# New planner limits for a mixed-attention kernel whose instruction order is made by a list scheduler

## Chip, cores and metric

The kernel runs on one core of one Trainium2 chip. The metric is device time in microseconds of one execution, as the median of several runs. A lower time is better.

## The reference

The input is one sequence of 2048 positions with 512 features. Two attention branches with 32 heads of 16 features each read it, and a gate per position mixes their outputs:

```python
def reference(A_x, A_wqkv, A_wo, B_x, B_wqkv, B_wo, gate_w):
    def _A_ref(x, wqkv, wo):
...
        scores = jnp.einsum("bhqd,bhkd->bhqk", q, k) * scale
        p = _softmax(scores, axis=-1)
        o = jnp.einsum("bhqk,bhkd->bhqd", p, v)
...
    def _B_ref(x, wqkv, wo):
...
        W, dil = 8, 2
...
        idx = pos[:, None] - off[None, :]
...
        logits = jnp.einsum("bhsd,bhswd->bhsw", q, kg) * scale
        logits = jnp.where(mask[None, None, :, :], logits, -1e9)
        attn = _softmax(logits, axis=-1)
        o = jnp.einsum("bhsw,bhswd->bhsd", attn, vg)
...
    x = A_x
    g = _sigmoid((x * gate_w).sum(-1, keepdims=True))
    a = _A_ref(x, A_wqkv, A_wo)
    b = _B_ref(x, B_wqkv, B_wo)
    return g * a + (1 - g) * b
```

Branch A is full attention: 32 heads times 2048x2048 scores, each of which needs an exponential. Branch B looks at 8 positions per query, two apart, so it is small next to A.

## The kernel before

**Items.** Branch A's scores are cut into 2048 *items*. An item is one head, 512 queries and 128 keys: a score matmul writes 128x512 f32 values into one PSUM bank (L1801), an engine takes the exponential into SBUF, and a value matmul multiplies the result with V and adds it to an accumulator bank (L1605). Thirty-two blocks of 64 items follow each other; a block is four heads by 512 queries by 16 key tiles. The four score matmuls of a group lie in four row strips of TensorE (PE), the four value matmuls in four column strips, so four run beside each other.

**Two ways to an exponential.** ScalarE (ACT) computes exps exactly, in one instruction for two or three items side by side (L1855); its two PSUM slots are three and two banks wide, and the planner may lend the third bank of the wide slot out, which makes that exp two items wide. VectorE (DVE) can take an item too: a first pass turns the scores into 16-bit integers that, read as f16, approximate the exponential (L1533), and for every batch of up to four items two later passes make shifted copies (L1539, in a tile called yb). The three pieces are summed by three value matmuls with weighted copies of V, so a DVE item has three value matmuls where an ACT item has one. Only 6 of the 16 key tiles (KD) may go to DVE, and none in the last items of a block.

**The rest.** Projections for Q, K and V of both branches run on PE (L881) and are evacuated by DVE, out of a pool of four banks called flex that DVE items and block accumulators use too. After a block DVE normalises it (L1628 on). Branch B multiplies Q with shifted K, sums, takes a softmax, writes weights and V to DRAM, reads them back in shifted form, and GpSimd (POOL) multiplies them (L1332); PE sums these products (L1350) and DVE evacuates them (L1355). Output tiles are projected on PE near the end, B's half first. When little PE work has been issued lately, the planner inserts matmuls on zeros to keep TensorE's activity up (L1517). A second, exact version of the kernel stands behind a flag and doesn't run with these inputs.

**What sets the order.** The order of all engines' instructions is made on the host, while the program is being built, by `run` (L1460 on). It is a list scheduler: it keeps a model time for each engine (`t`), takes the engine that is furthest behind, and lets it issue the best candidate. `p` counts items whose score matmul has been issued. Other work is a list of steps, each with an engine, a cost, predecessors, an item number before which it may not start (`rel`), one by which it is wanted (`due`), and a class for DVE. The chip's engines then run their queues in that order and wait for each other through semaphores; a wrong cost in the model can't break the result, but it can leave an engine waiting.

**The limits.** Eleven limits steer the choices. Each has five levels (`LEVELS`, L55), and a digit per stretch of 32 items picks the level (`STRETCH`, L68; 64 stretches). `tune(k)` (L1498) gives the level in force. What they do:

- `backlog`, `backlog_s`, `misc_slack` (L1724 to L1736, `d_wanted`): a DVE item is taken only while the DVE work that is queued or ready within 1.5 us costs less than `backlog` us, and while no step that needs a bank is due by `p + misc_slack`. `backlog_s` takes the place of `backlog` where only the lending of a bank is decided.
- `lend` (L1907): when the wide slot's third bank is lent: 1, if a DVE item is wanted; 2, if a step that needs a bank is due; 3, either; 4 and more, always.
- `grab` (L1913): how many DVE items may ride with one score burst. `alone` (L1978): the margin in time for a DVE item's score matmul by itself.
- `part_us` (L1948): after how many us a value group of fewer than four goes. `urgent` (L1946): other PE steps go ahead of value matmuls once due within so many items. `fit` (L1934): PE starts other work only if that ends no more than `fit` us after the next ACT slot is expected to come free.
- `port` (L1891): how much other DVE work must be at hand before POOL may start a product, because POOL and DVE's fast passes are kept apart in time by explicit dependencies.
- `order` (L1876): the rank of DVE's step classes: first transpose of a finished block, evacuations, first passes on items, later passes, background.

The two lines in which an item is taken or refused:

```python
            load = max(0.0, t["DVE"] - now) + sum(s.cost for s in ready if s.eng == "DVE")
            return load < tune("backlog" if flex else "backlog_s")
```

Of the kernel before, what the change touches and what calls it, by code (L numbers as in the profile page):

```python
# [55 lines left out]
    backlog=(1.5, 2.2, 3.0, 3.8, 5.0),  # L56
    backlog_s=(0.5, 1.0, 1.5, 2.2, 3.0),
    part_us=(1.5, 2.2, 3.0, 4.0, 6.0),
    misc_slack=(-20, -8, 0, 8, 20),
    urgent=(0, 4, 8, 16, 32),  # L60
    fit=(-0.2, 0.0, 0.2, 0.4, 0.6),
    port=(0.3, 0.6, 0.9, 1.2, 2.0),
    alone=(-9.0, -0.2, 0.0, 0.2, 9.0),
    grab=(0, 1, 4, 2, 1),
    lend=(0, 1, 3, 2, 7),
    order=((-1, 1, 0, 2, 3), (-1, 0, 2, 1, 3), (-1, 0, 1, 2, 3), (-1, 0, 1, 2, 1), (1, 0, 1, 2, 3)),
)
STRETCH = dict(  # L68
    backlog="4213224322422022220413433124322022122202222223242202222212220022",
    backlog_s="2202222312432222422021322322222202212222042122213222222022222323",  # L70
    part_us="2220421041243222243202020241242042211223124202210222222222222220",
    misc_slack="0004233313424222221242320140240224120321112121323222222242210222",
    urgent="2322222222200222222212213221431222034112012232322222222021222222",
    fit="2421222322244222322212212022422212421422222223222222222022222222",
    port="2223222202243220222020324222224422222202222222221322222222341322",
    alone="2211222122222114022222243221222222221322242231222232222233302222",
    grab="1222212222214222222222222222222224411342244213222222222422422422",
    lend="4220222222233202222224132222224232322212222244232122222242311422",
    order="2222432212022222320131412123232222203202222120223222222222222222",
)  # L80
SLOT_D = 3
D_LAST = 58
# [1957 lines left out]
```

## Time and profile before

| what | value |
|---|---|
| time, median of 4 runs | 736.44 us (735.89 to 736.94) |
| the profiled execution: its time | 736.56 us |
| the profiled execution: span from first to last instruction | 734.8 us |
| mean granted TensorE clock | 0.997 |
| DVE items (first passes, L1533) | 501 |
| exps on ACT, two items wide / three wide | 484 / 193 |
| ACT's exps, busy | 707.8 us |
| POOL's products of branch B (L1332) | 128, from 414.8 to 700.3 us |
| DMA | 48.53 MB, mean 66 GB/s |

The page gives busy time per engine as the union of its instructions' spans. ACT's and DVE's instructions overlap a little at their ends, so the mean of one instruction times their number is more than the busy time of the group; the distance between two starts is shorter than an instruction's span. PE's spans are modelled at their ends, and a busy PE is not PE at its peak. A group's line has the source line, engine, operation, tiles, shapes and count, then busy us, the mean ns of one, the engine's idle time just before them, and what ended it.

### The profile page before, as it was taken

What the parts mean: (1) busy time and instruction counts of PE and PEld (TensorE: products, weight loads), DVE (VectorE), ACT (ScalarE), POOL (GpSimd) and SP (SyncE); (2) the same over time, 40 slices, a digit from 0 to 9 for tenths busy, and PEclk for the clock granted to TensorE, in tenths of its full rate; (3) what the DMA queues carried; (4) which work ended last, traced back from release to release, by engine and by line L of the source; (5) the groups of instructions that cost most, each with busy time, mean ns of one, the idle gap of its engine ahead of it and who ended that gap; (6) DMA issues with size and microseconds to landing.
All of it is one profiled execution on the core that took longest, in us unless ns stands there. A gap on an engine that the chain in (4) does not pass through costs nothing.

```text
span 734.8 us, 20496 instructions
## 1 busy us (share of the span) xinstructions
PE 691.0 (94%) x8285; PEld 229.1 (31%) x8285; DVE 653.7 (89%) x1114; ACT 713.3 (97%) x691; POOL 204.6 (28%) x218
## 2 busy tenths in 40 slices
PE   8999999999999999999989998999999999999996
PEld 5333322333332232323222322232223323322333
DVE  6988889986799999998998998999889998899974
ACT  4999999999999999999999999999999999999994
POOL 3143000000002232123000336655543546361500
PEclk9999999999999999999999999999999999999998
DMA  6002000000100100001021455476444465374101
GB/s 166 3 18 70 10 17 9 1 2 2 39 2 14 26 1 3 6 1 38 2 74 72 115 110 153 113 169 163 116 122 125 122 156 130 81 173 121 37 24 35
DMA packets 63718, 48.53 MB, mean 66 GB/s; under 512 B 21760, under 2 KB 63232, under 8 KB 63488
## 3 DMA queue, kind: packets, MB, share of 16 engines
q1 hardware_dynamic: 62912, 45.70, 24.7%
q8 instruction: 67, 1.10, 0.7%
q0 software_dynamic: 288, 1.05, 0.5%
q10 hardware_dynamic: 416, 0.39, 0.2%
q14 instruction: 35, 0.29, 0.2%
HBM read 39.85 MB, written 5.26 MB: 61 GB/s over the span
## 4 chain that ended last, share of the span: by engine, by line
ACT 46%; PE 26%; issue 15%; DVE 9%; DMA 2%; SPq 1%; POOL 0%; ACTq 0%; POOLq 0%
ACT pt L1855 45%; PE fps L1801 10%; PE fps L1605 7%; PE fps L881 7%; DVE yb L1533 4%; DVE yb L1539 2%; DMA vw<-v_dram 1%; SPq L1300 1%; PE fps L1215 1%; SPq L948 1%; ACT er L1220 1%; PE fps L954 0%; PE fps L1350 0%; DVE t L1628 0%; DVE oT L1641 0%
## 5 line engine op out<-in xcount | busy, mean ns | idle before, releaser
L1855 ACT ACTIVATE pt<-fps 128x1024 bf16<-128x1024 f32 (+1 forms) x677 | 707.8, 1244 | 6.6 <-PE fps L1801 5.7
L1533 DVE TENSOR_SCALAR yb<-fps 128x512 int16<-128x512 f32 x501 | 325.6, 682 | 31.7 <-PE fps L1801 30.3
L1801 PE MATMUL fps<-qm,kT 32*128 32x512 bf16 x2048 | 309.9, 382 | 32.8 <-ACT pt L1855 24.4
L1605 PE MATMUL fps<-pt,vaug 128*32 128x512 bf16 (+1 forms) x1646 | 237.3, 373 | 0.7 <-DVE bq L1177 0.5
L1801 PEld LDWEIGHTS <-kT 32*128 32x128 bf16 x2048 | 95.0, 91 | 296.7 <-issue 289.8
L1539 DVE TENSOR_SCALAR yb<-yb 128x2048 int16<-128x2048 int16 (+3 forms) x270 | 169.0, 656 | 0.8
L1605 PE MATMUL fps<-yb,vaugw 128*32 128x512 f16 (+1 forms) x1060 | 160.2, 372 | 0.6 <-DVE yb L1539 0.5
L1332 POOL TENSOR_TENSOR er<-er,vw 128x512 bf16<-128x512 bf16 x64 | 72.7, 1154 | 136.0 <-DMA erb<-er_dram 69.2
L881 PE MATMUL fps<-xT,ww 128*32 128x512 bf16 (+2 forms) x1296 | 97.5, 381 | 0.2
L1605 PEld LDWEIGHTS <-vaug 128*32 128x32 bf16 x2176 | 66.7, 94 | 86.9 <-issue 75.3
L1605 PE MATMUL fps<-yb,vaug 128*32 128x512 f16 (+1 forms) x530 | 92.5, 372 | 0.0
L1332 POOL TENSOR_TENSOR erb<-erb,vw 128x512 bf16<-128x512 bf16 x64 | 72.4, 1155 | 60.7 <-DVE yb L1539 32.8
L1201 POOL TENSOR_TENSOR prod<-bq,bk 128x512 bf16<-128x512 bf16 x32 | 33.8, 1074 | 95.2 <-DVE yb L1539 65.8
L1605 PEld LDWEIGHTS <-vaugw 128*32 128x32 bf16 x1060 | 43.7, 95 | 35.7 <-issue 28.0
L1124 POOL DMA_DIRECT2D wAv<-in_A_wo_dram x1 | 0.8, 754 | 121.7 <-PE fps L881 121.7
L881 PEld LDWEIGHTS <-ww 128*32 128x32 bf16 x1296 | 23.8, 95 | 34.1 <-issue 28.8
L1201 DVE TENSOR_TENSOR prod<-bq,bk 128x2048 bf16<-128x2048 bf16 x24 | 29.3, 1241 | 0.2
L1628 DVE STREAM_TRANSPOSE t<-fps 128x512 f32<-128x512 f32 x32 | 22.7, 709 | 4.2 <-PE fps L1605 4.1
L1517 PE MATMUL fps<-wz 128*32 128x512 bf16 x157 | 21.5, 382 | 0.0
L909 DVE CAST vaug<-fps 128x384 bf16<-128x384 f32 (+1 forms) x24 | 12.2, 510 | 10.2 <-PE fps L881 10.1
L881 PE MATMUL fps<-woB,oB 128*32 128x512 bf16 x256 | 19.6, 383 | 0.3 <-DVE yb L1533 0.2
L881 PE MATMUL fps<-wAv,oT 128*32 128x512 bf16 x256 | 19.6, 384 | 0.1
(112 smaller groups left out, 281.1 us busy)
## 6 DMA issues: line engine op xcount, KB each, us to landing
vw<-v_dram SPq DMA_DIRECT2D x128, 128.0 KB, 3.2
er<-er_dram SPq DMA_DIRECT2D x128, 64.0 KB, 3.0
erb<-er_dram SPq DMA_DIRECT2D x128, 64.0 KB, 3.0
v_dram<-vs SPq DMA_DIRECT2D x16, 128.0 KB, 2.8
out_dram<-ob SPq DMA_DIRECT2D x15, 128.0 KB, 2.6
qm<-qs SPq DMA_DIRECT2D x112, 16.0 KB, 1.8
x_in<-in_A_x_dram SPq DMA_DIRECT2D x3, 512.0 KB, 6.6
ww<-in_B_wqkv_dram SPq DMA_DIRECT2D x12, 128.0 KB, 2.5
```

What stands on the lines that cost most here:

```text
L881: self.nc.tensor.matmul(out=out_ps[32 * c:32 * c + 32, 0:n], lhsT=lhsT_of(c), rhs=rhs, start=start, stop=stop, tile_position=(0, 32 * c))
L909: self.nc.vector.tensor_copy(out=self.vaug4[:, st0:st0 + nst, h0:h1, 0:DH], in_=self.misc[:, 0:nst * n].rearrange("p (t h e) -> p t h e", ...
L948: self.nc.sync.dma_start(out=self.qm[i % NQM][r][k:k + 16, :], in_=self.qs[i % 2][k:k + 16, :])
L1201: return e.tensor_tensor(out=pr[m % 2][:, a:b], in0=bq[ct][:, a:b], in1=bk[ct][:, o + a:o + b], op=ALU.mult)
L1332: return nc.gpsimd.tensor_tensor(out=st_["erb"][m % 4][:, g, :], in0=st_["erb"][m % 4][:, g, :], in1=st_["vw"][m % 2][:, g, :], op=ALU.mult)
L1517: nc.tensor.matmul(out=self.flex[acc[cur]][32 * j:32 * j + 32, :], lhsT=self.wz[:, 0:32], rhs=self.wz[:], start=False, stop=False, tile_po ...
L1533: return nc.vector.tensor_scalar(out=self.yb[bt["buf"]][:, 0, i * 512:(i + 1) * 512], in0=bank[:], scalar1=A, scalar2=1024.0 * (15.0 + PW_ ...
L1539: return nc.vector.tensor_scalar(out=y[:, k, 0:n], in0=y[:, 0, 0:n], scalar1=float(round(1024.0 * (PW_S[k] - PW_S[0]))), scalar2=None, op0 ...
L1605: nc.tensor.matmul(out=out, lhsT=v, rhs=r, start=start, stop=stop, tile_position=(0, 32 * j))
L1628: nc.vector.transpose(out=self.t1[:, par].rearrange("p a b -> p (a b)"), in_=self.flex[acc[b]])
L1801: nc.tensor.matmul(out=dst, lhsT=self.kT[ct % 2][32 * j:32 * j + 32, kt * 128:(kt + 1) * 128], rhs=self.qm[(4 * ct + qc) % NQM][par][32 * ...
L1855: nc.scalar.activation(out=self.pt[pi[0]][pi[1]][:, 0:n * 512], in_=self.aslot[si][:, 0:n, :].rearrange("p a b -> p (a b)"), func=ACT.Exp, ...
```

## The change

Only the digits of `STRETCH` change; `LEVELS`, the step list, the costs in the planner and the code stay. Before, every limit sits at level 2 in most stretches, and 240 of the 704 digits differ from that. After, every limit has one most common level, and 21 digits differ from it. In all, 527 of the 704 digits are others than before.

| limit | most common level before | after |
|---|---|---|
| backlog | 3.0 us | 2.2 us |
| backlog_s | 1.5 us | 2.2 us |
| part_us | 3.0 us | 1.5 us |
| misc_slack | 0 items | -8 items |
| urgent | 8 items | 0 items |
| fit | 0.2 us | 0.4 us |
| port | 0.9 us | 0.9 us |
| alone | 0.0 us | 0.0 us |
| grab | 4 | 4 |
| lend | 3 | 1 |
| order (transpose, evacuation, first pass, later pass, background) | -1, 0, 1, 2, 3 | 1, 0, 1, 2, 3 |

```diff
--- before.py
+++ after.py
@@ -66,17 +66,17 @@
     order=((-1, 1, 0, 2, 3), (-1, 0, 2, 1, 3), (-1, 0, 1, 2, 3), (-1, 0, 1, 2, 1), (1, 0, 1, 2, 3)),
 )
 STRETCH = dict(
-    backlog="4213224322422022220413433124322022122202222223242202222212220022",
-    backlog_s="2202222312432222422021322322222202212222042122213222222022222323",
-    part_us="2220421041243222243202020241242042211223124202210222222222222220",
-    misc_slack="0004233313424222221242320140240224120321112121323222222242210222",
-    urgent="2322222222200222222212213221431222034112012232322222222021222222",
-    fit="2421222322244222322212212022422212421422222223222222222022222222",
-    port="2223222202243220222020324222224422222202222222221322222222341322",
-    alone="2211222122222114022222243221222222221322242231222232222233302222",
-    grab="1222212222214222222222222222222224411342244213222222222422422422",
-    lend="4220222222233202222224132222224232322212222244232122222242311422",
-    order="2222432212022222320131412123232222203202222120223222222222222222",
+    backlog="1111111111131111111111111111111111111111111111111111211111111111",
+    backlog_s="3333333333333333333333333333333333333333333333333333133333333233",
+    part_us="0000010000040000000000000000000000000000000000000000000000000000",
+    misc_slack="1111111111111111111111111111111111111111111111111111111111111111",
+    urgent="0000000000000000000000000000000000000000000000000000000000000000",
+    fit="3333333333333333333333333333333333333333333333333333333333333332",
+    port="2222222222232222222222222222222222222222222222222222432222222222",
+    alone="2222221222122222222222222222222222322222222222222222122212222222",
+    grab="2222222222222222222222222222222222122221222222222222222222212222",
+    lend="1111111111111111111111111111111111011111111111111111111111111111",
+    order="4144444444444444444444444444444444444144444444444444444444444444",
 )
 SLOT_D = 3
 D_LAST = 58
```

## The prediction

> **What bounds the kernel now.** I read the page's table of engines first, then busy time cut into windows at every 32nd score matmul (the planner's own stretches), then the waits, then the chain of waits near the end.
>
> ```profile
> PE 691.0 (94%) x8285; PEld 229.1 (31%) x8285; DVE 653.7 (89%) x1114; ACT 713.3 (97%) x691; POOL 204.6 (28%) x218
> ```
>
> ScalarE (ACT) is busy for 97% of the span; its first exp starts at 9.15 us and its last ends at 724.47. Between them it has almost no hole, as the waits say (engine, line, releaser: total us, times, longest):
>
> ```profile
> ACT pt L1855 <- PE fps L1801: 5.7, 4, 3.9
> ...
> PE fps L1801 <- ACT pt L1855: 24.4, 84, 0.8
> ...
> PE fps L1801 <- DVE yb L1533: 3.8, 13, 0.7
> ```
>
> Of the 5.7 us, 3.9 are one hole at 14.54 us, in the start-up. Score matmuls wait for ACT far more than for VectorE (DVE). So the time is: a head, the exps that ACT has to do back to back, a tail of 10.3 us. A schedule can shorten it chiefly by giving ACT fewer items. There are 2048 items (128x512 scores each); ACT's shapes say how many it gets:
>
> ```profile
> L1855 ACT ACTIVATE pt<-fps 128x1024 bf16<-128x1024 f32 x484 | 489.0, 1119 | 4.7 <-PE fps L1801 3.9 <-PE fps L1605 0.4
> L1533 DVE TENSOR_SCALAR yb<-fps 128x512 int16<-128x512 f32 x501 | 325.6, 682 | 31.7 <-PE fps L1801 30.3
> ...
> L1855 ACT ACTIVATE pt<-fps 128x1536 bf16<-128x1536 f32 x193 | 300.6, 1557 | 1.9 <-PE fps L1801 1.8
> ```
>
> 484x2 + 193x3 = 1547 on ACT and 501 on DVE: 2048, so no record is missing here. **The room is in DVE.** Rows are one stretch each: its window, length, then busy us of PE, PEld, DVE, ACT, POOL, with PE clock, DMA share and GB/s at the end:
>
> ```profile
> 158.22:171.16 12.94, 11.95 (x164) 4.19 (x160) 10.52 (x20) 12.94 (x13) 0.00 (x0) 1.00 0.01 1
> 171.16:183.37 12.21, 11.04 (x149) 3.92 (x141) 7.22 (x13) 12.19 (x12) 0.00 (x0) 1.00 0.00 1
> ...
> 354.12:363.57 9.45, 9.15 (x92) 2.73 (x92) 8.74 (x16) 9.45 (x11) 0.00 (x0) 1.00 0.01 2
> 363.57:376.20 12.63, 11.86 (x143) 3.50 (x136) 12.60 (x21) 12.63 (x14) 0.00 (x0) 1.00 0.36 94
> ...
> 451.43:461.87 10.44, 9.04 (x97) 2.68 (x96) 10.44 (x18) 10.44 (x11) 6.23 (x6) 1.00 0.58 158
> ```
>
> ACT is full in all of them, DVE is not: in 171.16:183.37 it idles 12.21 - 7.22 = 4.99 us, while in 451.43:461.87 it idles nothing. Over the 60 stretches from 34.59 to 699.90 us DVE is busy 605.49 of 665.31 us, so it idles 59.8 us. The median stretch idles 0.65 us; the 21 that idle over 1 us hold 45.9 of the 59.8. These are places where a ready DVE was not given an item.
>
> **Prices.** One item moved from ACT to DVE: an exp of 1536 columns takes 1557 ns, one of 1024 takes 1119, so 512 columns are 0.438 us of ACT, and that comes off the span while ACT is full. DVE pays for its first pass and its share of the two later passes: all instructions on yb keep DVE busy 478.0 us for 501 items, 0.954 us each. So one item uses up 0.954 + 0.438 = 1.392 us of DVE idle time (the span shrinks under it too). PE pays two more value matmuls, as a DVE item has three passes and an ACT item one. The chain of waits in the tail (start, us, what) gives their price:
>
> ```profile
> 713.26 0.55 PE fps L881 x8
> ...
> 714.02 0.32 PE fps L1801 x2
> 714.34 0.98 PE fps L881 x16
> 715.32 0.32 PE fps L1801 x3
> ```
>
> Eight more matmuls cost 0.98 - 0.55 = 0.43 us, so two cost 0.11, and changing over between score and column matmuls costs about 0.55 - 0.43 = 0.12 us. PE is busy 669.4 of the 704.5 us between 20 and 724.5 us, so it has some 35 us of room.
>
> **The change part by part.** No operation, DMA, tile or byte is added or removed; what changes is where the planner puts them on each engine's queue and how items are shared out. I go by groups of limits.
>
> *Appetite for DVE items.* backlog (a take needs a DVE queue below this) goes from 3.0 us in most stretches to 2.2; backlog_s from 1.5 to 2.2; misc_slack from about 0 to -8, so that waiting projections and copies no longer stop a take until they are 8 items overdue. The first refuses takes when DVE is already loaded, the other two allow takes when it is not. Upper bound of the gain: if the 21 idle stretches fell to the median, 45.9 - 21x0.65 = 32.3 us of idle would go, 32.3/1.392 = 23 items, 10.2 us. If all 59.8 us went: 43 items, 18.8 us. Lower bound: the lower backlog starves DVE. The trace holds an experiment on that: 12 of the 60 stretches already have backlog at 2.2 or 1.5, and idle 1.23 us on average against 0.94 in the other 48. If all behaved so, 62x0.29 = 18 us more idle, 13 items fewer, +5.7 us. But 12 stretches with ten other limits mixed in prove little, and the 16 stretches with misc_slack at -8 or -20 point the other way: 0.79 us against 1.07. I take half of the 32.3 us: 16.2/1.392 = 12 items, **-5.3 us**, because idle time that comes from a full PE (V projections, 34 to 230 us) can't be filled by any limit.
>
> *Lending.* lend goes to 1: the third bank of ACT's wide slot is lent only when a DVE item wants it, no longer for projections too. Six items as two exps of three or three of two: from the union of all exps, 707.8 us = 193a + 484(a - 0.438), a = 1.359 and 0.921 us, so 2.718 against 2.763, 45 ns per six items. If the 145 or so narrow exps in the wide slot changed by a third, about 50x0.045/2 = 1 us either way. I take 0.
>
> *Order on PE.* part_us falls from 3.0 (mostly) to 1.5 us, urgent from 8 to 0, fit rises from 0.2 to 0.4: value matmuls go earlier, in groups of fewer than four, ahead of projections; other PE work may run 0.4 us past the moment a slot frees. Cover: 24.4 us over 84 waits, 0.29 us each, in which PE sat ready and ACT was late. If that cover is gone, a score burst is late by the extra 0.2 us; were that so at 5% of the 677 exps, +6.8 us. A value group of two in place of four wastes half of 0.22 us; if 76 groups (10% of about 760) were split, 76x0.22 = 17 us of PE's 35. Gain side: earlier value matmuls release yb buffers sooner, which is in the -5.3. I take 0 here.
>
> [...]
>
> *order and misc.* order puts the first transpose of a finished block beside the item passes instead of ahead: at most one pass, 0.68 us, later on 32 blocks, hidden as two other banks stand ready; uncovered, 32x0.68 = 22 us of bank time, not of span. port, alone and grab keep their most common level.
>
> *Branch B and the tail.* Later misc work delays branch B's chain, where POOL's products wait for DVE's passes (75.3 us in 33 waits). Its last evacuation starts at 701.3 us; the last output tiles' B half is finished on PE at about 724. The cover is some 20 us; 8 items of delay are 8x0.36 = 2.9 us. I take 0; uncovered, each us late is a us of span. The start-up hole of 3.9 us could shrink (down to 0) but the projections that fill it stay: 0.
>
> **Sum.** The profiled execution took 736.56 us, span 734.8 plus 1.8 around it; the median is 736.44. 736.4 - 5.3 = **731.1 us**.
>
> **Rivals.**
> 1. *The balance lands where it was* (240 of the old entries differ from one level, the new ones are nearly uniform, yet both feed the same rules): DVE items stay within about 3 of 501, 736.4 us. For it: the median stretch already idles only 0.65 us. Against: 45.9 us in 21 stretches.
> 2. *Starved DVE, slower.* Place: every stretch whose DVE queue runs at 2.2 to 3.0 us. A take is refused, the next chance is an exp later (about 1 us), DVE runs dry. It decides from 4 items fewer on; price 13 items, 742.1 us. For it: the 12 stretches above. Against: a queue of 2.2 us outlasts two exps.
> 3. *Branch B too late, slower.* If POOL's 75.3 us of waits for DVE grow by a third, its end moves 25 us, 5 past the cover: about 741.5 us, less whatever DVE gained. It decides from 20 us of delay on.
> 4. *Large gain*: idle of all stretches below the present median, 23 items or more, and the start-up hole closed: 736.4 - 10.2 - 3.9 = 722.3 us.
>
> **Chances.** Forecast 0.42 (its own range 726 to 735), no change 0.14, starved 0.22, B or a full PE 0.13, large gain 0.09. Faster by over 0.2% (1.5 us, about what a measurement of this kernel can tell from no change): 0.51; within: 0.14; slower: 0.35. The range 722 to 742 leaves out what lies beyond the two bounds, about 2 in 10.
>
> **What would show it.** Right: count of DVE first passes 507 to 520, ACT columns down by as many 512s, DVE idle in the middle near 44 us, ACT still without holes. Wrong: fewer than 498 first passes (rival 2); waits of ACT for score matmuls of 10 us or more (PE order); branch B's last evacuation behind 720 us or a tail well over 10.3 us (rival 3). The prediction fails at its root if the time moves while the item count stays.

## The result, and the profile after

The changed kernel takes 735.21 us (median of 40 runs, 731.05 to 737.98) against 736.44 us (62 runs, 735.22 to 739.40). The ratio of the times is 0.9979, with an interval of 0.9973 to 0.9985: 1.5 us faster by the ratio (1.2 us between the medians), where 5.3 us were forecast. The profiled execution is one of the longest, 737.94 us with a span of 736.2 us. The runs spread widely, and with TensorE's mean granted clock: the run at 0.997 took 731.05 us, the one at 0.987 took 737.98 us.

The page's engines, after:

```profile
PE 699.2 (95%) x8304; PEld 226.3 (31%) x8304; DVE 674.3 (92%) x1149; ACT 706.5 (96%) x704; POOL 205.8 (28%) x218
```

ACT has less to do (706.5 us against 713.3), DVE more (674.3 against 653.7). The groups by shape say how many items moved:

```profile
L1855 ACT ACTIVATE pt<-fps 128x1024 bf16<-128x1024 f32 x546 | 531.6, 1091 | 10.2 <-PE fps L1801 8.2 <-PE fps L1605 1.2
L1533 DVE TENSOR_SCALAR yb<-fps 128x512 int16<-128x512 f32 x526 | 340.3, 682 | 22.7 <-PE fps L1801 21.2
...
L1855 ACT ACTIVATE pt<-fps 128x1536 bf16<-128x1536 f32 x143 | 217.7, 1523 | 4.6 <-PE fps L1801 4.2
```

DVE has 526 items, 25 more, twice the 12 of the forecast; ACT has 690 exps in place of 677 (one of them a single item wide), of which 143 are three wide in place of 193. All exps together keep ACT busy for 700.7 us, 7.1 us less than before. So the work for the forecast gain is gone from ACT, and more; the span did not follow. ACT's waits, after, and then PE's:

```profile
ACT pt L1855 <- PE fps L1801: 12.4, 19, 4.0
```

```profile
PE fps L1801 <- ACT pt L1855: 16.0, 55, 0.6
PE fps L881 <- DMA ww<-in_B_wqkv_dram: 3.6, 1, 3.6
```

The second wait of PE is new: a projection waits 3.6 us for a weight load. The timeline shows it and what follows (start us, us, engine, line, what; in brackets the idle time before it):

```profile
58.73 0.40 PE L1605 MATMUL fps<-pt,vaug 128*32 128x512 bf16 x3
...
60.13 0.58 SPq L876 DMA_DIRECT2D ww<-in_B_wqkv_dram  x1
62.69 1.04 PE L881 MATMUL fps<-xT,ww 128*32 128x512 bf16 x8 [3.56 <-DMA ww<-in_B_wqkv_dram]
...
64.40 1.02 ACT L1855 ACTIVATE pt<-fps 128x1024 bf16<-128x1024 f32 x1 [3.96 <-PE fps L1801]
...
65.03 0.63 PE L1605 MATMUL fps<-yb,vaug 128*32 128x512 f16 x1
65.03 0.64 PE L1605 MATMUL fps<-yb,vaugw 128*32 128x512 f16 x2
...
65.30 0.69 DVE L1177 CAST bk<-fps 128x512 bf16<-128x512 f32 x1 [5.27 <-PE fps L881]
```

PE starts no matmul in those 3.56 us: the score matmuls behind the projection in its queue start at 63.67 us (1.0 us after it), and ACT stands for 4 us. Matmuls that took 0.40 us before the wait take 0.63 to 0.64 us after it. Busy time by window (us of PE, PEld, DVE, ACT, POOL, then PE clock, DMA share, GB/s) tells why:

```profile
59.00:61.25 2.25, 0.13 (x4) 0.00 (x0) 1.04 (x3) 1.44 (x2) 2.25 (x3) 1.00 0.10 23
61.25:68.08 6.83, 5.39 (x42) 1.04 (x45) 1.70 (x3) 2.69 (x3) 2.50 (x3) 0.52 0.08 19
68.08:75.00 6.92, 6.74 (x89) 1.90 (x81) 6.78 (x13) 6.53 (x7) 1.92 (x2) 0.98 0.06 14
```

The granted clock falls to half for 6.83 us, from 61.50 us on (so the middle row has 0.52), and ACT is busy for 2.69 us of the middle row. Two more falls of 3.41 us come at 481 and 645 us; the profile of before has none ahead of its tail (its clock is 1.00 from 8 to 724 us). Why the load is late stands on SP's queue, before and then after (start us, us, line, tile, number of DMAs):

```profile
37.23 10.53 SPq L1121 DMA_DIRECT2D gA<-gs  x16
47.88 4.94 SPq L948 DMA_DIRECT2D qm<-qs  x8
52.86 0.58 SPq L876 DMA_DIRECT2D ww<-in_B_wqkv_dram  x1
53.55 16.09 SPq L948 DMA_DIRECT2D qm<-qs  x16
```

```profile
37.78 11.00 SPq L1121 DMA_DIRECT2D gA<-gs  x16
48.89 11.19 SPq L948 DMA_DIRECT2D qm<-qs  x16
60.13 0.58 SPq L876 DMA_DIRECT2D ww<-in_B_wqkv_dram  x1
```

In both, 16 small DMAs of the gate hold SP's queue for some 11 us. They are issued inside a DVE step (`gate_t`, L1112), and the planner charges SP only for steps of its class DMA: in its account the queue is free. Before, the load of branch B's first K weights came behind one group of 8 q pieces; after, a q projection is done earlier, its 8 pieces get ahead of the load as well, and the load leaves 7.3 us later.

### The profile page after: what moved, and what is told of

The parts are those of the page before. It is cut to its first block, busy times and chain, and to the rows that moved or that the text cites. A ratio compares the mean times of both kernels' runs of the same rounds, so it can differ in the third digit from the quotient of the medians.

```text
span 736.2 us, 20619 instructions
## 1 busy us (share of the span) xinstructions
PE 699.2 (95%) x8304; PEld 226.3 (31%) x8304; DVE 674.3 (92%) x1149; ACT 706.5 (96%) x704; POOL 205.8 (28%) x218
## 4 chain that ended last, share of the span: by engine, by line
ACT 38%; PE 34%; issue 11%; DVE 11%; SPq 5%; DMA 1%; DVEq 0%; ACTq 0%
ACT pt L1855 37%; PE fps L1801 12%; PE fps L1605 11%; PE fps L881 7%; DVE yb L1533 4%; DVE yb L1539 2%; SPq L1300 2%; SPq L948 1%; SPq L1121 1%; PE fps L1350 1%; DVE prod L1201 1%; PE fps L1215 1%; DVE t L1637 0%; PE fps L954 0%; ACT er L1220 0%
## 5 line engine op out<-in xcount | busy, mean ns | idle before, releaser
L1855 ACT ACTIVATE pt<-fps 128x1024 bf16<-128x1024 f32 (+1 forms) x690 | 700.7, 1180 | 14.8 <-PE fps L1801 12.4
L1533 DVE TENSOR_SCALAR yb<-fps 128x512 int16<-128x512 f32 x526 | 340.3, 682 | 22.7 <-PE fps L1801 21.2
L1605 PE MATMUL fps<-pt,vaug 128*32 128x512 bf16 (+1 forms) x1618 | 248.3, 375 | 0.1
L1801 PEld LDWEIGHTS <-kT 32*128 32x128 bf16 x2048 | 90.8, 91 | 285.6 <-issue 278.5
L1539 DVE TENSOR_SCALAR yb<-yb 128x2048 int16<-128x2048 int16 (+3 forms) x280 | 176.4, 660 | 0.8
L1605 PE MATMUL fps<-yb,vaugw 128*32 128x512 f16 (+1 forms) x1116 | 164.2, 374 | 2.2 <-DVE yb L1539 2.1
L881 PE MATMUL fps<-xT,ww 128*32 128x512 bf16 (+2 forms) x1296 | 100.8, 387 | 4.6 <-DMA ww<-in_B_wqkv_dram 3.6
L1605 PE MATMUL fps<-yb,vaug 128*32 128x512 f16 (+1 forms) x558 | 100.0, 374 | 0.1
L881 PEld LDWEIGHTS <-ww 128*32 128x32 bf16 x1296 | 26.4, 96 | 37.6 <-issue 25.5
L881 PE MATMUL fps<-wAv,xT 128*32 128x128 bf16 (+1 forms) x512 | 18.3, 274 | 0.0
```

The source lines that it names most:

```text
L881: self.nc.tensor.matmul(out=out_ps[32 * c:32 * c + 32, 0:n], lhsT=lhsT_of(c), rhs=rhs, start=start, stop=stop, tile_position=(0, 32 * c))
L1533: return nc.vector.tensor_scalar(out=self.yb[bt["buf"]][:, 0, i * 512:(i + 1) * 512], in0=bank[:], scalar1=A, scalar2=1024.0 * (15.0 + PW_ ...
L1539: return nc.vector.tensor_scalar(out=y[:, k, 0:n], in0=y[:, 0, 0:n], scalar1=float(round(1024.0 * (PW_S[k] - PW_S[0]))), scalar2=None, op0 ...
L1605: nc.tensor.matmul(out=out, lhsT=v, rhs=r, start=start, stop=stop, tile_position=(0, 32 * j))
L1801: nc.tensor.matmul(out=dst, lhsT=self.kT[ct % 2][32 * j:32 * j + 32, kt * 128:(kt + 1) * 128], rhs=self.qm[(4 * ct + qc) % NQM][par][32 * ...
L1855: nc.scalar.activation(out=self.pt[pi[0]][pi[1]][:, 0:n * 512], in_=self.aslot[si][:, 0:n, :].rearrange("p a b -> p (a b)"), func=ACT.Exp, ...
```

## The experiments

**Theory Q**: the 25 items are worth some 7 us, and the late load with the half clock behind it eats most of that. **Rival P**: the new order on PE costs the gain in small holes all over. For the prediction's own steps: **J**, the limits only work together, against a gain of the appetite limits alone. Six runs (1 to 4 and 7) keep the plan of their kernel and move or add single instructions; the six with other digits (5 and 6) have new plans. Each ratio is to the kernel before, run alongside.

**1. The load early, in the changed kernel.**

```diff
         def b1_open():
-            self.xin.release()
+            self.load_w("B", "k", 0); self.xin.release()
...
-                wl = self.dma(lambda ct=ct, kind=kind: self.load_w("B", kind, ct), 6.0, rel=R0 + 16 * n - 44)
+                wl = self.dma(lambda ct=ct, kind=kind: (ct, kind) == (0, "k") or self.load_w("B", kind, ct), 6.0, rel=R0 + 16 * n - 44)
```

> The changed schedule, item for item the same on PE, ACT, DVE and POOL; only the load of branch B's first K weights is put on SP's queue ahead of the gate's 16 small DMAs instead of behind them and 16 q pieces. Theory Q (the 25 items that moved to DVE are worth about 7 us, and one weight load that is late by 3.6 us, with the TensorE clock at half for some 7 us behind it, eats most of it): the 3.6 us wait of PE and the half clock near 61 us are gone, ACT idles some 6 us less in the first 75 us, time 730 to 732 us. Rival P (the order on PE, more value groups of fewer than four, costs the gain in small holes all over): the wait goes, but the time falls by under 1.5 us, to 733.7 us or more.

Measured: 730.42 us, ratio 0.9925 (0.9909 to 0.9941). ACT's waits fall to

```profile
ACT pt L1855 <- PE fps L1801: 5.9, 13, 1.6
```

and the first 75 us have no half clock. Theory Q holds: with the same items on the same engines, one load further up the queue is worth 0.54% (0.9979 to 0.9925), some 4 us of median. P falls as the main cause.

**2. The same in the kernel before** (the same edit).

> The kernel before with the same early load. There the load was issued at 52.9 us and PE did not wait for it. Theory Q: no change, 736.4 us within 0.7. If an early load helps by itself (a freer queue for what comes behind), it would gain here as well, 2 us or more.

Measured: 736.16 us, ratio 1.0007 (0.9995 to 1.0018). An early load is worth nothing by itself; before, it was in time.

**3. The load late, in the kernel before.**

```diff
-                wl = self.dma(lambda ct=ct, kind=kind: self.load_w("B", kind, ct), 6.0, rel=R0 + 16 * n - 44)
+                wl = self.dma(lambda ct=ct, kind=kind: (ct, kind) == (0, "k") or self.load_w("B", kind, ct), 6.0, rel=R0 + 16 * n - 44)
...
-                    qdone[(ct, sc)] = self.dma(lambda ct=ct, sc=sc: self.q_split(ct, sc), T_LAND, deps=qd,
+                    qdone[(ct, sc)] = self.dma(lambda ct=ct, sc=sc: (self.q_split(ct, sc), (ct, sc) == (0, 2) and self.load_w("B", "k", 0)), T_LAND, deps=qd,
```

> The kernel before with the same weight load put behind one more group of 8 q pieces on SP, as the changed schedule has it by its own order. Nothing else moves. Theory Q: the load is issued near 58 us instead of 52.9, PE waits 2 to 3 us for it, TensorE's clock may fall to half behind the wait, and the time goes to 739 to 742 us. Rival P: no change, 736.3 us within 1.

Measured: 742.07 us, ratio 1.0073 (1.0058 to 1.0089). The timeline is that of the changed kernel again:

```profile
59.33 0.58 SPq L876 DMA_DIRECT2D ww<-in_B_wqkv_dram  x1
...
61.85 1.04 PE L881 MATMUL fps<-xT,ww 128*32 128x512 bf16 x8 [3.70 <-DMA ww<-in_B_wqkv_dram]
```

with the clock at half from 60.98 us for 6.83 us. The same displacement costs 5.4 us (0.73%) in the old schedule.

**4. The wait kept, TensorE kept busy.** In the changed kernel, 64 matmuls on zeros ahead of the waiting projection.

```diff
-                        ("PE", 2 * MM, lambda ct=ct, kind=kind, sc=sc:
+                        ("PE", 2 * MM, lambda ct=ct, kind=kind, sc=sc: [self.mm4(self.misc, lambda c: self.wz[:, 0:32], self.wz[:], start=True, stop=True) for _ in range(16 * ((ct, kind, sc) == (0, "k", 0)))] and None or
                             self.proj_mm(self.w_tiles[("B", kind, ct)], (0, 1), sc)),
```

> The changed kernel with its late weight load as it is; only TensorE computes 64 matmuls on zeros (some 3.5 us) just ahead of the matmuls that wait for the load, so that it waits busy instead of idle. The lateness stays, the half clock behind it should not come. Theory Q with its two shares (in the changed kernel's profile stretches 3 and 4 take 28.6 us, with the early load 22.8: 3.6 us of wait and 2.2 us of half clock): no half clock near 61 us, 732.5 to 734 us. If the wait alone costs everything: 735 us. If the half clock costs nearly everything: 731 us.

Measured: 732.06 us, ratio 0.9948 (0.9933 to 0.9962). The projection still starts only when the load has landed (61.62 us):

```profile
58.04 3.63 PE L881 MATMUL fps<-wz 128*32 128x512 bf16 x64
...
61.66 0.62 PE L881 MATMUL fps<-xT,ww 128*32 128x512 bf16 x8
```

but its eight matmuls take 0.62 us in place of 1.04, and the clock stays full up to the tail. From 0.9979 to 0.9948 is the half clock (0.31%, 2.3 us), from there to 0.9925 the wait (0.23%, 1.7 us). The intervals don't show which part is larger, and the split is approximate: with the load early the runs' mean clock is a little lower than here (median 0.996 against 0.9975), so that kernel has more half clock at other places.

**5. Groups of limits in the old table.** Digits of before, except those of one group, which are the new ones: backlog, backlog_s, misc_slack and lend; then part_us, urgent and fit.

```diff
-    backlog="4213224322422022220413433124322022122202222223242202222212220022",
+    backlog="1111111111131111111111111111111111111111111111111111211111111111",
...
```

```diff
-    part_us="2220421041243222243202020241242042211223124202210222222222222220",
+    part_us="0000010000040000000000000000000000000000000000000000000000000000",
...
```

> The table of before with the new digits for backlog, backlog_s, misc_slack and lend alone; part_us, urgent, fit, order and the rest as before. The prediction's sum put the whole gain (-5.3 us, 12 items more) on these four: by that 728 to 733 us and 510 or more items on DVE. Rival S (starved DVE, named in the prediction): fewer than 490 items, and 0.44 us more for each that is missing. Rival J (the limits only work together, with the order on PE): fewer items than 501 here.

> The table of before with the new digits for part_us, urgent and fit alone. The prediction put 0 on them: 736.4 us within 2, 501 items within 5. Rival J (only together): fewer items here too. Rival P (these three make small holes): ACT waits for score matmuls over 10 us and the time is 738 us or more with the item count unchanged.

Measured: 799.66 us, ratio 1.0875 (1.0855 to 1.0896), with 422 items; and 745.14 us, ratio 1.0126 (1.0111 to 1.0141), with 493. Each group alone loses items in the old table, as J says. In the second run the clock is full (granted 1.00), the exps take 714.0 us, 6.1 more than before, and ACT's idle time is 7.7 us, 2.4 more: mostly more work for ACT, not holes. Its waits for score matmuls are 7.9 us, below the 10 of P. The first run's size has another cause as well, to be read in two windows:

```profile
345.00:456.21 111.21, 101.47 (x1023) 31.14 (x1023) 98.80 (x164) 111.21 (x109) 33.15 (x30) 1.00 0.37 95
456.21:565.44 109.23, 109.13 (x433) 21.03 (x432) 7.43 (x13) 103.07 (x103) 7.57 (x7) 0.50 0.08 20
```

For 109 us TensorE runs at half clock, DVE takes no item (its 13 instructions are other work) and ACT alone works through them. 201 score matmuls are issued there; the same 201 by number go with 52 DVE items in the kernel before, so 27 of the 79 missing items lie elsewhere. TensorE does some 14 matmuls in 3.41 us there, against 31 in the row above. The planner plans with 1.9 times the PE costs while it has issued little PE work (`slow`); that such a plan kept the clock at half is not shown. So this run shows J only together with run 6.

**6. Groups of limits on an even table.** All digits 2; then 2 with the four appetite limits new in all stretches; then the three PE limits as well; then order as well, which is the new table without its 21 odd digits. The last three have the early load.

```diff
+    backlog="1111111111111111111111111111111111111111111111111111111111111111",
+    backlog_s="3333333333333333333333333333333333333333333333333333333333333333",
...
```

> Every limit at level 2 in every stretch: the table of before without its 240 odd digits. Expected 485 to 490 items on DVE and 742 to 750 us, if the 240 digits of before bought items as the 21 of after do; 737 us or less if they bought nothing.

> Every limit at level 2 except backlog, backlog_s, misc_slack and lend, which stand at their most common new level in all stretches; early load. Against the run with everything at level 2 (486 items, 747.5 us) the prediction's step gives 12 items and 5.3 us to this group: 498 items, 742 us. If the group is worth all of the uniform table's gain: 516 items, 731.5 us. If it is worth nothing without the order on PE: 747 us or more.

> The same with part_us, urgent and fit at their most common new level too, so that only order stands apart from the uniform table of the run at 731.5 us. The prediction put 0 on these three and 0 on order: by that the same time as with the appetite group alone. If the order on PE matters: several us less than that run. What is left to 731.5 us is what order brings.

> The new table without its 21 odd digits (each limit at its most common new level in all 64 stretches), with the early load. It shows what the choice stretch by stretch adds. If the level changes carry the gain: 515 items or so on DVE, 733 to 736 us. If the 21 digits carry it: 505 items or fewer, 738 us or more.

Measured, with what one profiled execution of each shows (ACT idle: between its first and last exp; half clock: in the same stretch):

| kernel | time us | ratio (interval) | DVE items | exps (three wide) | exps busy us | ACT idle us | half clock us |
|---|---|---|---|---|---|---|---|
| before | 736.44 | 1 | 501 | 677 (193) | 707.8 | 5.3 | 0 |
| after | 735.21 | 0.9979 (0.9973 to 0.9985) | 526 | 690 (143) | 700.7 | 14.3 | 13.7 |
| after, load early | 730.42 | 0.9925 (0.9909 to 0.9941) | 526 | 690 (143) | 700.1 | 7.9 | 3.4 |
| all at level 2 | 747.48 | 1.0137 (1.0121 to 1.0153) | 486 | 676 (211) | 714.5 | 11.9 | 20.5 |
| + appetite | 751.32 | 1.0213 (1.0194 to 1.0232) | 498 | 691 (168) | 711.5 | 16.2 | 37.5 |
| + PE limits | 744.78 | 1.0136 (1.0111 to 1.0161) | 504 | 697 (150) | 711.2 | 11.6 | 13.7 |
| + order (even new table) | 731.46 | 0.9931 (0.9917 to 0.9945) | 516 | 689 (154) | 703.9 | 5.7 | 0 |

The appetite limits do bring the 12 items that the forecast gave them, and the time still rises. In the profiles half clock grows with it, from 20.5 to 37.5 us, and ACT's idle time by 4.3 us, while the exps fall by 3.0 us; that the clock is the cause is not shown. (The kernel with all at level 2 has the load at its usual place, so this one step changes that as well.) The PE limits bring 6 more items and 6.5 us, order, added last, another 12 items and 13.3 us (by the ratios 5.7 and 15.1 us), and only then is the half clock gone. No run has order without the others, so these shares hold for this sequence. The 21 odd digits of after bring 10 items more, and 0.0006 of ratio, which the intervals don't separate from nothing; the 240 of before brought 15 items and 10 to 11 us.

**7. What is left of half clock.** With the load early, the profile still has one fall ahead of the tail, at 636.99 us, just behind the start of a value group that waits 1.1 us for DVE:

```profile
633.21 0.33 DVE L1633 RECIPROCAL rc<-t 128x32 f32<-128x32 f32 x1
...
633.28 0.39 PE L1605 MATMUL fps<-pt,vaug 128*32 128x512 bf16 x2
633.28 2.27 POOL L1332 TENSOR_TENSOR erb<-erb,vw 128x512 bf16<-128x512 bf16 x2 [11.06 <-DVE yb L1533]
...
633.58 0.91 DVE L1634 TENSOR_TENSOR rc<-rc,gA 128x32 f32<-128x32 f32 x1
...
634.52 1.57 DVE L1637 TENSOR_TENSOR t<-t,rc 128x512 bf16<-128x512 f32 x1
...
636.02 0.68 DVE L1539 TENSOR_SCALAR yb<-yb 128x2048 int16<-128x2048 int16 x1
...
636.75 0.43 PE L1605 MATMUL fps<-yb,vaugw 128*32 128x512 f16 x4 [1.08 <-DVE yb L1539]
```

POOL's product starts after 11 us of idle time and runs beside DVE's normalisation, whose two steps (L1634 and L1637) take 0.91 and 1.57 us where they take 0.19 to 0.20 and 0.69 us at the 14 other places of this profile. In the profile of the changed kernel the same two steps take 1.14 and 1.58 us at 640.77 and 641.95 us, again beside a product (from 640.71 us, 2.27 us long), and 0.19 to 0.23 and 0.69 us at the 14 other places; why they are longer beside it is not shown. Two runs tried to keep the clock up. One puts 20 matmuls on zeros ahead of that group:

```diff
+                        if p == 1816 and not self.log.get("kept"):
+                            self.log["kept"] = 1
+                            for _ in range(5):
+                                for j in [j for j in range(4) if (cur, j) in started and jleft[(cur, j)] > 0]:
+                                    nc.tensor.matmul(out=self.flex[acc[cur]][32 * j:32 * j + 32, :], lhsT=self.wz[:, 0:32], rhs=self.wz[:],
+                                                     start=False, stop=False, tile_position=(0, 32 * j))
                         mms = [emit_pv_one(j, now) for j in av]
```

> The changed schedule with the early load, and 20 matmuls on zeros (1.1 us) ahead of the one value group near 636 us that waits 1.1 us for a late pass of DVE; in the early-load run TensorE's clock fell to half for 3.4 us right there. If half clock behind a wait is what is left to gain: no half clock near 637 us, 729 to 730 us and a narrower spread than 729.1 to 732.5 us. If the clock falls elsewhere or the lost time is the wait itself: 730.4 us within 0.7.

Measured: 729.70 us, ratio 0.9917 (0.9903 to 0.9930), the fastest kernel here, though its interval overlaps that of the early load alone. The fall near 637 us is gone from the profile; another of 3.4 us is at 423.8 us. The other run fills the empty column strips of every partial value group:

```diff
+                        for j in [j for j in range(4) if j not in av and cur in acc and (cur, j) in started and jleft[(cur, j)] > 0]:
+                            nc.tensor.matmul(out=self.flex[acc[cur]][32 * j:32 * j + 32, :], lhsT=self.wz[:, 0:32], rhs=self.wz[:],
+                                             start=False, stop=False, tile_position=(0, 32 * j))
```

> The changed schedule with the early load; in every value group that holds fewer than four matmuls, the column strips that stay empty get a matmul on zeros, which runs beside the others. Nothing else moves. If TensorE's clock falls because the partial groups leave the array too empty, no half clock is left before the tail and every run lies near 729 us, as the fastest of the early-load runs. If idle time of PE sets the clock and not empty strips: half clock still comes now and then, and the median stays at 729.7 to 730.4 us. If the additional matmuls delay PE: 732 us or more.

Measured: 731.52 us, ratio 0.9935 (0.9923 to 0.9948), 392 matmuls more, half clock for 3.41 us twice. The time lies between the second and the third case expected. Filling the empty strips did not keep the clock up.

## Why the prediction was wrong

**The bound was right.** ACT's exps set the time: in all fourteen profiles the span is exps busy plus ACT idle plus 20.0 to 22.1 us. (In the timeline of before the exps run from 9.40 to 724.72 us, 0.25 us later than the prediction has them, so the tail is 10.1 us; no sum rests on it.)

**The count of items was too low, the price too high.** The forecast took half of the idle stretches' 32.3 us as usable, 12 items; 25 came, and DVE's idle time in the middle 60 stretches fell to 42.2 us where "near 44" was forecast. An item brought less than 0.438 us: 25 items took 7.1 us off the exps (0.29 us each), as 50 exps became narrower and 13 more are needed. That is the lending term, put at 0 with a bound of 1 us: it took 45 ns for one exp more. By the two shapes' spans, 13 exps more cost 13 x 0.243 us (1119 - 2 x 438 ns) = 3.2 us, and 25 x 0.438 - 3.2 = 7.8 us, which is near the 7.1 and 7.7 us measured after and with the early load.

**The step that failed is the sentence on DMAs.** "No operation, DMA, tile or byte is added or removed; what changes is where the planner puts them on each engine's queue": that was said and then priced at nothing. Cover was asked for score bursts and for branch B's tail, 20 us ahead of the end; SP's queue in the first 60 us, where a load had some 3 us to spare before (landed at 55.4 us, first used at about 58), was not looked at. Moved behind 8 DMAs, it cost 4 us by run 1 against after, 5.4 us by run 3. None of the rivals had this place. The mark set for the order on PE, ACT waiting 10 us or more for score matmuls, did show (12.4 us), but for a wait of PE on a load and the clock behind it. Rival 3 did not come: branch B's last evacuation starts at 685.9 us, earlier than before.

**The clock was left out.** The forecast never priced TensorE's clock, as the profile of before showed it full (1.00 from 8 to 724 us); run 4 puts some 2.3 us on the one fall behind the wait. Of the profiled executions' difference (span +1.4 us), the exps give -7.1 and ACT's idle time +9.0; the remaining -0.5 lies in head, tail and ACT's other work.

**The shares were put on the wrong groups.** All -5.3 us went to the appetite limits, 0 to the order on PE and 0 to order. Run 6, in the sequence tried there, gives appetite its 12 items but no time, the PE limits 6.5 us, order 13.3 us. Rival 2, starvation by a lower backlog, did not happen on the even table. With the load early, the changed schedule takes 730.42 us, close to the 731.1 forecast, but by twice the items at two thirds of the price: the agreement is a coincidence of two errors.

**Open.** Why the clock falls at 481 us in one execution and at other places in the next was not settled. The fall at 645 us has the run-up of the one in run 7: at 641.9 us L1637 takes 1.58 us beside a POOL product, and PE waits 1.3 us behind it. That the spread of 731 to 738 us comes from the clock is read from the runs' mean clocks (over the 42 on record they correlate with the time at -0.78), not shown. Half clock is not always dear: one execution of run 2 had a mean clock of 0.946, which is some 80 us at half, and took 738.71 us, 2.6 us above that run's median.

## What to carry to other kernels

When a planner rearranges a kernel, list every DMA whose place in its queue moved and compare its landing with its first use, also those that are issued from inside another engine's step and cost the planner nothing. A load that PE waited 3.6 us for cost 4 to 5.4 us here, with half clock behind the wait; matmuls on zeros in front of the wait took the half clock away and left some 1.7 us. Limits tuned together should be tried together: here two groups of them, each alone in the old table, lost time where the whole table won.

## What the runs showed of the hardware

Ahead of the tail, half clock came for 6.83 us once and for 3.41 us twice in the changed kernel's profile, for 3.41 us with the early load, for 6.83 us in run 3 and for 109.23 us in run 5; the longer two are 2 and 32 times 3.41 us. The falls in the changed kernel have no one length of pause ahead of them: the first, at 61.50 us, came 2.4 us into the wait of 3.6 us, at 481 us the clock fell where PE's longest single pause in the 7 us ahead was 0.5 us, at 645 us where it was 1.3 us. In the 3.41 us ahead of these three falls PE was busy for 1.04, 2.86 and 2.02 us (length, then us of PE, PEld, DVE, ACT, POOL, then PE clock, DMA share, GB/s):

```profile
58.09:61.50 3.41, 1.04 (x18) 0.20 (x7) 1.95 (x5) 2.35 (x3) 2.78 (x3) 1.00 0.10 25
477.92:481.33 3.41, 2.86 (x28) 1.02 (x30) 3.41 (x6) 3.41 (x4) 2.05 (x2) 1.00 0.84 224
641.76:645.17 3.41, 2.02 (x20) 0.69 (x20) 3.38 (x5) 2.42 (x4) 2.12 (x3) 1.00 0.67 164
```

What makes the clock fall was not shown. In run 5 PE counted as busy for 109.13 of 109.23 us at half clock, with 433 matmuls, whose ends are modelled, and the clock did not come back in that time. With 64 matmuls on zeros (3.63 us) in place of the 3.56 us of idle time the clock stayed full up to the tail (run 4).
